# Two DMAs in place of four for the rows of maxima, and the last attention quad in an order of its own

## The chip, the cores and the metric

The kernel runs on one core of a Trainium2 chip. The metric is the device time of one execution in microseconds (us). TensorE (PE; PEld is its weight load), VectorE (DVE), ScalarE (ACT), GpSimd (POOL) and the DMA queue of SyncE (SP) each work through their own instructions in the order in which they were written, and wait for one another only through semaphores.

## The reference, cut to what matters

One transformer block on x, 2048 tokens of 576 features, in float32:

```python
mod = (silu(c) @ w_mod).reshape(1, 6, 1, -1)            # sa, ca, ga, sb, cb, gb
h = layernorm(x) * (1 + ca) + sa
q = (h @ wq) as 32 heads of 18;  k = h @ wk;  v = h @ wv    # one key and value head for all
p = softmax(q k^T * 18 ** -0.5);  x = x + ga * (p v as 576 features) @ wo
h = layernorm(x) * (1 + cb) + sb
x = x + gb * (gelu(layernorm(h) @ w1 + b1) @ w2 + b2)       # w1 is 576 x 4608
```

## The kernel before, in words

Numbers are kept as pairs: a value is rounded to the matmul type (the high part), and the rest (the low part) is a tile of its own; a product of pairs is three matmuls. All order is written out by hand: each engine executes in the order of the Python code.

**Attention.** The tokens are four blocks (`tb`) of 512; the heads are eight groups of four. One block with one group is a *quad*, so there are 32, numbered `n` from 0. In a quad:

- `st_mm` (L941) makes 64 score matmuls of 128 keys by 512 tokens, for two groups `g` of partitions (tokens S0 and S1 in the tables of order). Their weights are a piece of `KS`, their operand is `QST[n]`, 64 partitions for each group. Each goes to a bank of PSUM, and ACT writes its exponential into `P` (L943).
- `pv_mm` (L931) multiplies a key tile of `P` (four score outputs) with V and adds it up in one bank, `psC`. A token `V4` is one whole key tile, `V3` three quarters of one. It runs two key tiles behind the scores (`LAG`).
- Seven PSUM banks go round in a ring (`bank`). A matmul takes the oldest, or a later one by the number of `+` behind its token, and waits until the bank's last reader is done.
- Softmax needs each row's maximum before its quad begins. The maxima of quad n+1 are found in quad n: score products with the queries as weights (M0, M1, R1 at L327, X1 at L951), reduced by DVE (L963, L961) or passed through ACT (L954). `smax_fin1` (F1) joins them, and `smax_fin2` (F2) turns them with PE (L365), and writes the negated maxima as high and low part into `ms` (ACT L367, DVE L368). DMAs on SP (L372) carry `ms` into two rows of each partition group of `QST[n+1]`, rows 54 and 55 and rows 118 and 119, where the score matmuls add them in. So the first score matmul of a quad waits for these DMAs.
- `post_quad` divides by the softmax's sum in steps: copy `psC` to `O` (ACT L748, as soon as the last `pv_mm` of the quad is issued), then the tokens T1, RC, T2, OS (transpose L751, reciprocal and product L754 and L755, transpose L757, split L767 and L768).
- A token `WO` is an output-projection piece: 14 matmuls (L733) for 128 tokens and half of the features, and an add on DVE (L737). There are 24 for the first three blocks. Quads 9 to 30 have one each, quad 30 has another one at its very end, and the last quad has one. Behind the 24th, `RW` reloads the last block of rows of the output weights (SP L1029), which the last block of tokens uses.

**The last quad** (n = 31) has no maxima to find. Its order is eight times the same pattern of four to six scores and a key tile at a time (`LASTW`, `LAST`).

**After it** come the output products of the last block: `wo_tile(t, k0, k1)` makes 24 matmuls (k 0 to 3) and 6 (k = 4, which needs the last quad's result) for 128 tokens. Tiles 0, 1 and 2 come at once, tile 3 (`rest`) between the first MLP products. At the same time `post_quad` runs for the last quad, on ACT and DVE alone, and `form` makes the MLP's operands from the normalized rows `yr`: for an operand such as T1, `=T1` is a difference of blocks (L1062), `+T1` its high part on ACT (L1069), `-T1` its low part (L1071), on DVE, or on POOL for the last two (T4, B22).

**The MLP** runs 36 rounds `v` (18 pieces of the hidden features for each half of the tokens) with seven products (A11, S2, S3, A12, S1, A22, S4; L1158). ACT and DVE make the gelu of their results (`gelu`, L1167 to L1173); POOL casts it and forms sums for the second layer (`sums`, L1178, L1179, L1234 to L1241), whose products `fc2s` (L1261) start one round later. `b2_scaled` (POOL, L641 and L642) scales the second bias row `b2g`; its first reader in this stage is L694.

Of the kernel before, what the change touches and what calls it, by code (L numbers as in the profile page):

```python
# [8 lines left out]
F32 = mybir.dt.float32  # L9
# [6 lines left out]
NB = 4  # L16
TB = S // NB
NT = TB // 128
KD = 5
NQ = H // 4  # L20
NQT = NB * NQ
# [3 lines left out]
R3 = 3 * DH  # L25
# [7 lines left out]
def block_kernel(ctx: ExitStack, tc, x, wqkv, wo, w1, b1, w2, b2, c, wmod, ident_in, out):  # L33
    nc = tc.nc
    ve, ac, po, pe, sy = nc.vector, nc.scalar, nc.gpsimd, nc.tensor, nc.sync
# [17 lines left out]
    def psB(): return bank() if RING else PS["t"].tile([128, 512], F32, name="psB", bufs=PS["b"])  # L53
# [4 lines left out]
    def bank(rank=0):  # L58

        b = RING.pop(rank)  # L60
        RING.append(b)
        return PS["t"].tile([128, 512], F32, name="bk%d" % b, bufs=1)
# [73 lines left out]
    QST = {}  # L136
# [226 lines left out]
    def smax_fin2(n, rank=0):  # L363
        p = bank(rank) if RING else psB()
        pe.transpose(p[:16, :128], MR.pop(n), ident)  # L365
        ms = pa.tile([16, 2, 128], F32R, name="ms")
        ac.activation(ms[:, 0], p[:16, :128], AF.Copy, scale=-1.0)  # L367
        ve.scalar_tensor_tensor(ms[:, 1], p[:16, :128], -1.0, ms[:, 0].bitcast(F32), op0=ALU.mult, op1=ALU.subtract)  # L368
        for g in range(2):
            for s in range(2):  # L370
                r = 64 * g + R3 + s
                sy.dma_start(QST[n][r:r + 1].rearrange("o p (t c) -> o (p t) c", c=128).bitcast(F32),  # L372
                             ms[8 * g:8 * (g + 1), s].bitcast(F32))


    for t in range(NT):
# [77 lines left out]
    for tb in range(NB):  # L454
        nz = big() if tb + 1 < NB else None
        for i, m in enumerate((4, 0, 1, 2, 3)):
# [27 lines left out]
            if tb < 2:  # L484
                for _ in range(NSTAT[tb][i]):
                    ln1_stats(*stats.popleft())
                for _ in range(NAPPLY[tb][i]):
                    b, t = applies.popleft()
# [15 lines left out]
    WO, YR, ATT, B2 = {}, {}, {}, {}  # L504
# [135 lines left out]
    def b2_scaled(b2g):  # L640
        po.tensor_mul(b2g, b2g, BC[:, 2, :])  # L641
        po.tensor_scalar(b2g, b2g, 2.0, None, op0=ALU.mult)  # L642
        return b2g
# [74 lines left out]
        po.tensor_tensor(R[:, 5:7], R[:, 5:7], R[:, 0:2], op=ALU.add)  # L718
        yield

    def wo_mm(tb, t, h2, p, k0, k1):
        A = ATT[tb]
        cs = slice(288 * h2, 288 * (h2 + 1))
        for k in range(k0, k1):
            w = 128 if k == KD - 1 and tb == NB - 1 else 126
            ah, al = (A[:w, i, 128 * t:128 * (t + 1)] for i in (k, KD + k))
            wh, wl = (WO[i][:w, k, cs] for i in "hl")
            if k < KD - 1 or tb == NB - 1:
                terms = [(ah, wh), (ah, wl), (al, wh)]
            else:  # L730
                terms = [(ah, wh), (al[:5 * DH], wl[:5 * DH])]
            for i, (a, b) in enumerate(terms):
                pe.matmul(p[:, :288], a, b, start=(k == 0 and i == 0), stop=(k == KD - 1 and i == len(terms) - 1))  # L733

    def wo_add(tb, t, h2, p):
        X = XT[:, NT * tb + t, 288 * h2:288 * (h2 + 1)]
        ve.tensor_tensor(X, p[:, :288], X, op=ALU.add)  # L737

    def wo_piece(tb, t, h2, p):
        wo_mm(tb, t, h2, p, 0, KD)  # L740
        wo_add(tb, t, h2, p)
# [137 lines left out]
    def tail_parts(o, tail, d, e=po):  # L879

        e.tensor_tensor(d, tail[:, 0], tail[:, 1], op=ALU.subtract)
        for x, y in ((o[:, :2], tail), (o[:, 2], d)):
# [18 lines left out]
            M1 S1+ S0 M0 S1 M0 V3 R1 S1 M0 M1+ S0 S1+ S0 V4 S1 T2 OS M0 X1++ M0 S1+ M0 WO S0 M1 S0 M1 S0 M1 V3  # L901
            S1 S0 M1 S0 M0 X1 V3 S1 M0 M1+ M0 S1+ S0 V4 M0 S1+ S0 S1 S0+ R1+ M0 V4 S0+ S1 M0 M1++ M1 S0+ V3 S0
            R1 M0+ F1 S1 S0 X1+ V4 M0 S1 M0 S1+ S0+ M1 F2 V3 S0+ R1 S0+ S1 M0 S1 M0 V3 M0 X1 S1 M0+ S1 R1+ S0 V3""".split()
    LASTW = "S0 S1 S0 S1 S0 S1 WO V4 S0 S1 V4".split()
    LAST = "S0 S1 S0 S1 V4 S0 S1 S0 S1 V4".split()
    P, PVt = {}, {}
    posts = []
    fill = deque([late_weights()])
# [1 line left out]
    def step(q):  # L910
        if q:
            try:
                return next(q[0])
            except StopIteration:
                q.popleft()
# [64 lines left out]
    def wo_next(rank):  # L980
        tb, t, h2 = pieces.popleft()
        wo_piece(tb, t, h2, bank(rank))
        for _ in range(2):
            if held[0] == "T":
                held[0] = step(fill)
        if h2 and tb < 2:
            fill.append(ln2_rows(tb, t))

    pq = 0
    for n in range(NQT):  # L990
        ns = [0, 0]
        if n < NQT - 1:
            order = QUADW if n > NQ else QUAD
            if n == NQT - 2:
                order = order + ["WO"]
        else:
            order = []
            for d in range(8):
                order += LASTW + ["RW"] if d == 4 else LAST
                order += {1: ["T1"], 2: ["RC"], 4: ["T2"], 5: ["OS", "V4"]}.get(d, [])  # L1000
        if n < NQT - 1:
            names = [tok[:2] for tok in order]
            kf, kr = (sum(int(tok[1]) for tok in order[:names.index(a)] if tok[0] == "V") // 4 for a in ("F2", "RC"))
            quiet = kf - 2, kf - 1, kr - 1
        for tok in order:
            rank = tok.count("+")
            tok = tok.rstrip("+")
            if tok[0] == "V":
                g = int(tok[1])
                while g:  # L1010
                    i = min(g, 4 - pq % 4)
                    if pq >= LAG:
                        pv_mm(*divmod((pq - LAG) // 4, 16), pq % 4, pq % 4 + i)
                    pq, g = pq + i, g - i
                    if pq % 4 == 0:
                        between(*divmod(pq // 4 - 1, 16))
            elif tok[0] == "S":
                g = int(tok[1])
                st_mm(n, ns[g] // 2, g, ns[g] % 2, rank)
                ns[g] += 1  # L1020
            elif tok in maxima:
                unit = next(maxima[tok], None)
                if unit:
                    mx_mm(*unit, tok[0], int(tok[1]), rank)
            elif tok == "WO":
                wo_next(rank)
            elif tok == "RW":
                for i, w in enumerate("hl"):
                    sy.dma_start(WO[w][:, KD - 1, :].bitcast(F32), woscr[i])  # L1029
            elif tok[0] == "F":  # L1030
                smax_fin1(n + 1) if tok == "F1" else smax_fin2(n + 1, rank)
            elif n:
                if next(posts[0], 0) == 0:
                    posts.pop()
        if n == NQT - 1:
            W1["r"] = per.tile([128, 40, 128], F32R, name="w1a", tag="big", bufs=3)
            load_w1(0, " ".join(OPS) + " tails")
# [36 lines left out]
    form = op_pieces(YR[0], ve)  # L1074
    RING.clear()
    open_ps("3", 4)
    wop = {}

    def wo_tile(t, k0, k1):
        if t not in wop:  # L1080
            p = psA() if t != 2 else None
            wop[t] = [psB()[:, :288] if t == 2 else p[:, h2, :288] for h2 in range(2)], p
        for h2 in range(2):
            wo_mm(NB - 1, t, h2, wop[t][0][h2], k0, k1)
        if k1 == KD:
            o, p = wop[t]
            if p is None:
                for h2 in range(2):
                    wo_add(NB - 1, t, h2, o[h2])
            else:  # L1090
                Xv = XT[:, NT * (NB - 1) + t, :].rearrange("p (a b) -> p a b", a=2)
                ve.tensor_tensor(Xv, p[:, :, :288], Xv, op=ALU.add)

    for t in range(3):
        wo_tile(t, 0, KD - 1)
    todo = deque(("+B11 +T2", "-B11 =T3 +B21 +T3", "-T2 -T3", "-B21"))
    form(todo.popleft())
    for _ in posts.pop():
        form(todo.popleft())
    for w in todo:  # L1100
        form(w)
    pxp.__exit__(None, None, None)
    tl = ctx.enter_context(tc.tile_pool(name="tl", bufs=1, side="right", reuse_waits="tile"))
    TL.append(tl.tile([128, 4, TB], F32R, name="opt"))
    px = ctx.enter_context(tc.tile_pool(name="mx", bufs=1, side="right", reuse_waits="tile"))
    form("+t0 -t0")
    for t in range(3):
        wo_tile(t, KD - 1, KD)
    form("+t1 =T4 =T1 +T1 -t1 -T1")
    rest = deque((3, k, k + 1) for k in range(KD))  # L1110
    B2["b"] = load_b2()
# [233 lines left out]
    def t_(mid=None):  # L1345
        between2[0] = mid
        step(f2)

    def s_():
        step(sm)  # L1350
# [5 lines left out]
                gens.remove(gen)  # L1356

    form = op_pieces(YR[0], po)
    b2_scaled(B2["b"])
    mark = [None]  # L1360

    for v in range(NV):
        nxt = (v + 1) % NG
        if v == NG - 1:
            while fill:
                step(fill)
            form = op_pieces(YR[1], po)

        def more(half="", first="", room=False):

            if v in (0, NG - 1, NG):
                form(first if v == 0 else half if v == NG - 1 else {"+T4": "-T4 +T1 -B22", "-T4": "-T1 -t1"}.get(first, ""))
            elif v > NG + 1 and fill:
                step(fill)
            elif 0 < v < NG and fill and (room or mark[0] != "T" or v == NG - 2):
                mark[0] = next(fill[0], "end")
                if mark[0] == "end":
                    fill.popleft()
            if v == 0 and rest:
                for _ in range(2):  # L1380
                    if rest:
                        wo_tile(*rest.popleft())
                if not rest:
                    wo_end()
# [33 lines left out]
        g_()  # L1418
        s_()
        more("+T3 +B21", "-B22", True)  # L1420
        t_()
        g_()
        bd = psB()
# [95 lines left out]
```

## Time and profile before

| | |
|---|---|
| median of 3 runs | 2237.01 us (2236.53 to 2237.12) |
| profiled execution | 2234.55 us, of which the span from first to last instruction is 2232.4 us |
| score matmuls L941 (attention) | from 128.1 to 1376.4 us |
| first MLP product L1158 | 1392.25 us |
| granted TensorE clock | 0.998 |
| busy | PE 99%, PEld 65%, DVE 86%, ACT 74%, POOL 68% |

In a row of the timeline the first number is the start in us, the second the time until the group's last instruction ends; then come the engine, the line, the operation, `out<-in`, shapes and a count; `[0.56 <-DMA qst<-ms]` is the engine's idle time just before and what ended it. PE ends are modelled, so a busy PE is not PE at its peak. A quad's score matmul takes two rows of 64 partitions in pairs: S0 and S1 run beside each other.

### The profile page before, as it was taken

The page shows a single profiled execution, that of the slowest core. Times are in us where ns is not written, and L with a number is a line of the kernel's source. Part 1 is how long each engine was busy: PE and PEld are TensorE (multiplying, and loading weights), DVE is VectorE, ACT ScalarE, POOL GpSimd, SP SyncE. Part 2 cuts the span into 40 slices and gives each one's busy share as a digit, 9 for nine tenths or more (in the row PEclk, how much of TensorE's full clock was granted, in tenths as well). Part 3 has the DMA queues.
Part 4 walks back from the last instruction along what each step waited for, and adds up shares of the span by engine and source line. Part 5 has one row for each costly group of instructions (what it writes and reads, how often), then busy time and mean ns, then how long its engine had stood idle before and what let it go on. Part 6 is the DMA issues. An engine that isn't in the chain of part 4 may idle for free.

```text
span 2232.4 us, 46436 instructions
## 1 busy us (share of the span) xinstructions
PE 2203.2 (99%) x16806; PEld 1453.9 (65%) x16806; DVE 1927.3 (86%) x3415; ACT 1646.1 (74%) x3145; POOL 1528.5 (68%) x1761
## 2 busy tenths in 40 slices
PE   8999999999999999999999999999999999999999
PEld 6655555544544445444454445888888898988898
DVE  7599999999999999999999982887888878888887
ACT  5579999999999999999999997444444544343443
POOL 6653466666776686687676630888888867877776
PEclk9999999999999999999999999999999999999999
DMA  6232143433333333333333321666666646676663
GB/s 232 86 128 92 38 139 108 142 123 118 124 119 118 114 129 104 106 133 103 109 129 112 126 70 60 200 179 177 180 179 175 191 126 182 182 216 187 179 184 123
DMA packets 184776, 308.01 MB, mean 138 GB/s; under 512 B 19711, under 2 KB 75407, under 8 KB 184549
## 3 DMA queue, kind: packets, MB, share of 16 engines
q1 hardware_dynamic: 184405, 304.91, 43.8%
q8 instruction: 133, 2.18, 0.4%
q14 instruction: 94, 0.77, 0.1%
q10 hardware_dynamic: 144, 0.15, 0.0%
HBM read 200.97 MB, written 93.79 MB: 132 GB/s over the span
## 4 chain that ended last, share of the span: by engine, by line
PE 88%; DVE 2%; POOL 2%; DMA 1%; ACT 1%; issue 0%; SPq 0%; DVEq 0%; POOLq 0%; ACTq 0%
PE psC L931 22%; PE psB L1158 18%; PE psA L1261 16%; PE bk L941 15%; PE bk L327 10%; PE bk L733 2%; PE bk L951 2%; PE psA L1295 1%; DMA qst<-ms 1%; DVE mx L963 1%; PE psA L733 1%; POOL r L802 0%; PE psB L256 0%; POOL r L863 0%; PE bk L365 0%
## 5 line engine op out<-in xcount | busy, mean ns | idle before, releaser
L943 ACT ACTIVATE P<-bk 128x512 f32<-128x512 f32 x2048 | 1066.5, 625 | 44.5 <-PE bk L327 18.4
L963 DVE TENSOR_REDUCE mx<-bk 128x1 f32<-128x512 f32 x1476 | 935.0, 682 | 51.5 <-PE bk L327 38.9
L941 PE MATMUL bk<-qst,KS 64*128 64x512 f32 x2048 | 597.2, 432 | 10.4 <-DMA qst<-ms 7.9
L327 PE MATMUL bk<-KS,qst 64*128 64x512 f32 x1722 | 590.1, 437 | 0.9
L931 PE MATMUL psC<-P,V 128*32 128x256 f32 (+3 forms) x6776 | 572.2, 433 | 1.0 <-ACT O L748 1.0
L941 PEld LDWEIGHTS bk<-qst,KS 64*128 64x128 f32 x2048 | 295.0, 184 | 284.0 <-ACT P L943 159.3
L1158 PE MATMUL psB<-ops,w1a 128*128 128x512 f32 x1512 | 393.8, 396 | 0.2 <-DVE h L1173 0.2
L327 PEld LDWEIGHTS bk<-KS,qst 64*128 64x128 f32 x1722 | 271.8, 184 | 130.3 <-ACT P L943 59.2
L1158 PEld LDWEIGHTS psB<-ops,w1a 128*128 128x128 f32 x1512 | 270.1, 188 | 46.6 <-DVE h L1173 0.6
L931 PEld LDWEIGHTS psC<-P,V 128*32 128x32 f32 x6776 | 152.3, 108 | 192.8 <-issue 158.3
L1267 DVE TENSOR_TENSOR XT<-psA,XT 128x576 f32<-128x576 f32 x330 | 241.7, 753 | 18.6 <-PE psA L1261 13.2
L1261 PEld LDWEIGHTS psA<-w2s,big 128*128 128x128 f32 x1584 | 223.0, 188 | 13.9 <-POOL big L1235 2.5
L1261 PE MATMUL psA<-w2s,big 128*128 128x288 f32 x1584 | 230.5, 294 | 0.0
L1171 ACT ACTIVATE psB<-gs 128x512 f32<-128x512 f32 x144 | 86.7, 602 | 127.9 <-DVE gs L1170 127.8
L1235 POOL TENSOR_TENSOR big<-s,big 128x512 fp32r<-128x512 f32 x132 | 171.0, 1296 | 10.6
L1167 ACT ACTIVATE h<-psB,b1t 128x512 f32<-128x512 f32 x144 | 98.1, 681 | 102.1 <-PE psB L1158 81.4
L961 DVE CUSTOM_DVE_ANT_0 xc<-bk,xc 128x512 f32<-128x512 f32 x246 | 167.3, 680 | 2.8 <-PE bk L327 1.7
L954 ACT ACTIVATE xc<-bk 128x512 f32<-128x512 f32 x246 | 151.4, 616 | 0.1
L768 POOL TENSOR_TENSOR os<-O,os 128x512 fp32r<-128x512 f32 x31 | 39.9, 1288 | 148.6 <-ACT os L767 148.1
L1170 DVE SCALAR_TENSOR_TENSOR gs<-psB,h 128x512 f32<-128x512 f32 x144 | 98.6, 684 | 39.9 <-ACT psB L1168 39.9
L802 POOL TENSOR_TENSOR r<-r,r 128x256 fp32r<-128x256 f32 (+1 forms) x162 | 122.0, 753 | 13.0
L1176 ACT ACTIVATE big<-h 128x512 fp32r<-128x512 f32 x39 | 24.7, 634 | 133.7 <-DVE h L1173 133.7
(219 smaller groups left out, 3277.9 us busy)
## 6 DMA issues: line engine op xcount, KB each, us to landing
w1a<-w1scr SPq DMA_DIRECT2D x252, 256.0 KB
w2s<-w2sum SPq DMA_DIRECT2D x132, 288.0 KB
w1scr<-r SPq DMA_DIRECT2D x126, 256.0 KB
w2s<-w2scr SPq DMA_DIRECT2D x76, 288.0 KB
w2scr<-r SPq DMA_DIRECT2D x72, 288.0 KB
w2sum<-r SPq DMA_DIRECT2D x72, 288.0 KB
qst<-qscr SPq DMA_DIRECT2D x192, 72.0 KB
w1a<-w2scr SPq DMA_DIRECT2D x33, 288.0 KB
```

The lines of the kernel that those rows point to most:

```text
L327: pe.matmul(o, QST[n][64 * g:64 * g + 64, p, 128 * qt:128 * (qt + 1)], KS[64 * g:64 * g + 64, 512 * kb:512 * (kb + 1)], start=True, stop=True)
L802: po.tensor_tensor(o[:, n:2 * n], src, o[:, :n].bitcast(F32), op=ALU.subtract)
L931: pe.matmul(PVt[n][32 * j:32 * (j + 1), cs], V[:, kc, :], t[:, j, cs], start=(kc == 0 and h0 == 0), stop=(kc == 15), skip_group_check=True)
L941: pe.matmul(t, KS[64 * g:64 * g + 64, 128 * kc:128 * (kc + 1)], QST[n][64 * g:64 * g + 64, i, :], start=True, stop=True)
L943: ac.activation(P[n, kc][:, 2 * i + g, :], t, AF.Exp, scale=SCALE)
L954: ac.activation(XC[-1], t, AF.Relu)
L961: ve.tensor_tensor_reduce(c, t, c, 1.0, -3.0e38, ALU.add, ALU.max, o)
L963: ve.tensor_reduce(o, t, axis=AX.X, op=ALU.max)
L1158: pe.matmul(o, x, y, start=(first and i == 0), stop=(i == len(terms) - 1), skip_group_check=True)
L1235: po.tensor_tensor(unit(u, 1), x, unit(u, 0).bitcast(F32), op=ALU.subtract)
L1261: pe.matmul(p[:, i, :288], x[:, ts_], W2S[k][:, y], start=(bool(first) and q == 0), stop=(q == 2), skip_group_check=True)
L1267: ve.tensor_tensor(o, p[:, :, :288], o, op=ALU.add)
```

## The change

Three things change.

**The rows of maxima.** `smax_fin2` issues two DMAs, one for the high and one for the low part; each writes row 54 + s of both partition groups at once.

**The last quad.** Both `WO` pieces that stood at the end of quad 30 and in the last quad stand inside the last quad now, and two tokens `WP` each make 12 of the 24 products of tile 2 of the last block (k 0 to 3, half of the features), added to the rows by DVE; the rest of that tile starts its sum at k = 4. The products with V come in groups of two key tiles or more.

**Between attention and MLP.** The forms of T2, T3 and B21 move behind the last steps of `post_quad`, the products with k = 4 stand ahead of the low parts of T3 and B21, and `b2_scaled` moves from ahead of the MLP into round 0.

```diff
-        for g in range(2):
-            for s in range(2):
-                r = 64 * g + R3 + s
-                sy.dma_start(QST[n][r:r + 1].rearrange("o p (t c) -> o (p t) c", c=128).bitcast(F32),
-                             ms[8 * g:8 * (g + 1), s].bitcast(F32))
+        for s in range(2):
+            r = R3 + s
+            sy.dma_start(QST[n][r:r + 65:64].rearrange("g p (t c) -> g (p t) c", c=128).bitcast(F32),
+                         ms[:, s].bitcast(F32))
...
-    def wo_mm(tb, t, h2, p, k0, k1):
+    def wo_mm(tb, t, h2, p, k0, k1, end=KD, first=0):
...
-                pe.matmul(p[:, :288], a, b, start=(k == 0 and i == 0), stop=(k == KD - 1 and i == len(terms) - 1))
+                pe.matmul(p[:, :288], a, b, start=(k == first and i == 0), stop=(k == end - 1 and i == len(terms) - 1))
...
-    LAST = "S0 S1 S0 S1 V4 S0 S1 S0 S1 V4".split()
+    LAST = """S1 S0 S1 S0 V8 S1 S0 T1 S1 S0 RC S1 S0 WO S0 S1 S0 T2 S1 V5 S1 S0 S1 S0 S1 OS S0 V11 S0 S1 S0 S1 S0
...
+    part = deque((0, 1))
...
-            if n == NQT - 2:
-                order = order + ["WO"]
...
+            elif tok == "WP":
+                h2 = part.popleft()
+                p = psB()
+                wo_mm(NB - 1, 2, h2, p, 0, KD - 1, KD - 1)
+                wo_add(NB - 1, 2, h2, p)
...
-            wo_mm(NB - 1, t, h2, wop[t][0][h2], k0, k1)
+            wo_mm(NB - 1, t, h2, wop[t][0][h2], k0, k1, first=KD - 1 if t == 2 else 0)
...
-    for t in range(3):
+    for t in range(2):
         wo_tile(t, 0, KD - 1)
-    todo = deque(("+B11 +T2", "-B11 =T3 +B21 +T3", "-T2 -T3", "-B21"))
+    todo = deque(("+B11 +T2", "", "", "-B11"))
     form(todo.popleft())
     for _ in posts.pop():
         form(todo.popleft())
-    for w in todo:
-        form(w)
+    form("-T2 =T3 +T3 +B21")
+    for t in range(3):
+        wo_tile(t, KD - 1, KD)
+    form("-T3 -B21")
...
-    for t in range(3):
-        wo_tile(t, KD - 1, KD)
...
-    b2_scaled(B2["b"])
...
         more("+T3 +B21", "-B22", True)
+        if v == 0:
+            b2_scaled(B2["b"])
```

PE where quad 30 ends and the last quad begins. L941 is a score matmul, L931 a product with V (four matmuls of 512 tokens are one key tile), L733 an output piece. Before:

```order
L931 MATMUL psC<-P,V 32x384 x4
L733 MATMUL bk_20642<-wos,big 128x288 x14
L941 MATMUL bk_20659<-qst,KS 128x512
L941 MATMUL bk_20662<-qst,KS 128x512
L941 MATMUL bk_20665<-qst,KS 128x512
L941 MATMUL bk_20668<-qst,KS 128x512
L931 MATMUL psC<-P,V 32x512 x4
L941 MATMUL bk_20676<-qst,KS 128x512
L941 MATMUL bk_20679<-qst,KS 128x512
L941 MATMUL bk_20682<-qst,KS 128x512
L941 MATMUL bk_20685<-qst,KS 128x512
L931 MATMUL psC<-P,V 32x512 x4
```

The same place of the change (lines above the products are one lower, so L733 is L732):

```order
L931 MATMUL psC<-P,V 32x384 x4
L941 MATMUL bk_20579<-qst,KS 128x512
L941 MATMUL bk_20582<-qst,KS 128x512
L941 MATMUL bk_20585<-qst,KS 128x512
L941 MATMUL bk_20588<-qst,KS 128x512
L931 MATMUL psC<-P,V 32x512 x8
L941 MATMUL bk_20602<-qst,KS 128x512
L941 MATMUL bk_20605<-qst,KS 128x512
L941 MATMUL bk_20610<-qst,KS 128x512
L941 MATMUL bk_20613<-qst,KS 128x512
L941 MATMUL bk_20620<-qst,KS 128x512
L941 MATMUL bk_20623<-qst,KS 128x512
```

The output piece ahead of the first scores is gone (it stands behind the last of these rows now), and the two key tiles that quad 30 still owes come together.

PE where the last quad ends and the MLP begins (L1158 is an MLP product). Before:

```order
L941 MATMUL bk_20958<-qst,KS 128x512
L941 MATMUL bk_20961<-qst,KS 128x512
L931 MATMUL psC<-P,V 32x512 x8
L733 MATMUL psA<-wos,big 128x288 x48
L733 MATMUL psB<-wos,big 128x288 x24
L733 MATMUL psA<-wos,big 128x288 x12
L733 MATMUL psB<-wos,big 128x288 x6
L1158 MATMUL psB<-ops,w1a 128x512 x6
```

Of the change:

```order
L732 MATMUL bk_20897<-wos,big 128x288 x12
L941 MATMUL bk_20912<-qst,KS 128x512
L941 MATMUL bk_20915<-qst,KS 128x512
L941 MATMUL bk_20918<-qst,KS 128x512
L941 MATMUL bk_20921<-qst,KS 128x512
L931 MATMUL psC<-P,V 32x512 x16
L732 MATMUL psA<-wos,big 128x288 x60
L732 MATMUL psB<-wos,big 128x288 x6
L1159 MATMUL psB<-ops,w1a 128x512 x6
```

Between the last product with V and the first MLP product there were 90 output products and are 66; the other 24 stand in the last quad, the second twelve of them in the first row here.

POOL from the last quad into the MLP's round 0. Before:

```order
L768 TENSOR_TENSOR os<-O,os 128x512
L641 TENSOR_TENSOR b2g<-b2g,BC 128x576
L642 TENSOR_SCALAR b2g<-b2g 128x576
L1071 TENSOR_TENSOR ops<-yr,ops 128x1024 x2
L1178 CAST gt_21202<-h 128x512
```

Of the change:

```order
L767 TENSOR_TENSOR os<-O,os 128x512
L1072 TENSOR_TENSOR ops<-yr,ops 128x1024 x2
L640 TENSOR_TENSOR b2g<-b2g,BC 128x576
L641 TENSOR_SCALAR b2g<-b2g 128x576
L1179 CAST gt_21144<-h 128x512
```

The two bias instructions stood ahead of the low parts of T4 and B22; they stand between these and the first cast of the gelu now.

More of the change, by code (lines that the diff above doesn't have):

```diff
@@ L903, in block_kernel @@
             R1 M0+ F1 S1 S0 X1+ V4 M0 S1 M0 S1+ S0+ M1 F2 V3 S0+ R1 S0+ S1 M0 S1 M0 V3 M0 X1 S1 M0+ S1 R1+ S0 V3""".split()
-    LASTW = "S0 S1 S0 S1 S0 S1 WO V4 S0 S1 V4".split()
-    LAST = "S0 S1 S0 S1 V4 S0 S1 S0 S1 V4".split()
+    LAST = """S1 S0 S1 S0 V8 S1 S0 T1 S1 S0 RC S1 S0 WO S0 S1 S0 T2 S1 V5 S1 S0 S1 S0 S1 OS S0 V11 S0 S1 S0 S1 S0
+            S1 WO RW S1 S0 S0 S1 S0 S1 V8 S0 S1 S0 S1 S0 S1 V8 S1 S0 S1 S0 S0 S1 WP S0 S1 S0 S1 V8 S0 S1 S0 S1
+            S0 S1 V8 S0 S1 S0 S1 S0 S1 WP S0 S1 S0 S1 V12""".split()
     P, PVt = {}, {}
@@ L993, in block_kernel @@
             order = QUADW if n > NQ else QUAD
-            if n == NQT - 2:
-                order = order + ["WO"]
-        else:
[L997 to L1000, printed above, removed]
+        else:
+            order = LAST
         if n < NQT - 1:
@@ L1008, in block_kernel @@
             if tok[0] == "V":
-                g = int(tok[1])
+                g = int(tok[1:])
                 while g:
```

## Prediction

> **What bounds the kernel now.** I read the page first (the chain that ended last), then the waits, then the timeline around the quad boundaries and from the last quad into the MLP.
>
> ```profile
> PE 88%; DVE 2%; POOL 2%; DMA 1%; ACT 1%; issue 0%; SPq 0%; DVEq 0%; POOLq 0%; ACTq 0%
> ```
>
> PE carries the chain, and the 1% of DMA, about 22 us, stands there beside `qst<-ms`, the rows of maxima. Of all waits only one stops PE itself for long:
>
> ```profile
> PE bk L941 <- DMA qst<-ms: 7.9, 13, 1.4
> ```
>
> Thirteen times, 7.9 us in all, the first score matmul of a quad waits for those rows. The timeline where quad 29 ends shows such a stop, and the chain the DMA that ends it:
>
> ```profile
> 1301.64 2.88 SPq L372 DMA_DIRECT2D qst<-ms  x4
> 1303.78 0.60 ACT L954 ACTIVATE xc<-bk 128x512 f32<-128x512 f32 x1
> 1304.34 0.85 PE L931 MATMUL psC<-P,V 128*32 128x384 f32 x8
> 1305.75 0.46 PE L941 MATMUL bk<-qst,KS 64*128 64x512 f32 x1 [0.56 <-DMA qst<-ms]
> 1306.25 0.60 ACT L943 ACTIVATE P<-bk 128x512 f32<-128x512 f32 x1 [0.41 <-PE bk L327]
> 1306.29 3.22 DVE L963 TENSOR_REDUCE mx<-bk 128x1 f32<-128x512 f32 x5 [0.65 <-PE bk L327]
> ```
>
> ```profile
> 1303.89 1.77 DMA qst<-ms
> ```
>
> Four issues begin at 1301.64, the fourth at about 1303.89, so 0.75 us apart; the fourth lands 1.77 later, at 1305.66, and the score matmul starts at 1305.75. PE had been done at 1305.19. In that gap PE, DVE (0.65) and ACT (0.41) all stand, so it is lost time for all three.
>
> **The rows of maxima: 32 x 2 DMAs less.** With two DMAs the second is issued at 1301.64 + 0.75 = 1302.39 and lands at 1304.16 if it takes the same 1.77. PE ends at 1305.19, so the stop is gone with 1.0 us to spare. What is late next is the matmul's PSUM bank; its last reader is the L954 above, done at 1304.38, so it costs nothing. The price of the new form isn't in the trace: each DMA carries twice the bytes into two partitions. From below I put the 0.75 and 1.77 as they are, from above the two doubled (1.5 and 3.54, a rival below); I take the first, since the cover of 1.0 us swallows more than half of 1.77 again.
>
> How much of the stops comes back? At other boundaries:
>
> ```profile
> 1262.15 2.84 SPq L372 DMA_DIRECT2D qst<-ms  x4
> 1103.17 2.93 SPq L372 DMA_DIRECT2D qst<-ms  x4
> 1106.35 0.85 PE L931 MATMUL psC<-P,V 128*32 128x384 f32 x8
> 1107.33 0.47 PE L941 MATMUL bk<-qst,KS 64*128 64x512 f32 x1
> 1142.71 2.87 SPq L372 DMA_DIRECT2D qst<-ms  x4
> 1222.54 2.93 SPq L372 DMA_DIRECT2D qst<-ms  x4
> 1226.76 0.47 PE L941 MATMUL bk<-qst,KS 64*128 64x512 f32 x1 [0.66 <-ACT P L943]
> ```
>
> The score matmul starts 4.11 us after the issue at 1301.64, 4.16 at 1103.17, 4.22 at 1222.54: a constant of the DMA, whatever the timeline names, so the 0.66 here counts as well. There are 21 such boundaries (at the ends of quads 9 to 29); the other seven stop for about 0.13 (1107.33 less 1107.20), where DVE had layer-norm statistics to do and PE was late by itself. In all 7.9 + 0.66 + 7 x 0.13 = 9.5 us. A check on back-pressure: the quad that began with the short stop, DVE some 0.4 behind, took 1142.71 - 1103.17 = 39.54 from issue to issue; one that began with the long one took 1301.64 - 1262.15 = 39.49. So 0.05 of about 0.42 is given back, one part in eight. **Gain: 0.9 x 9.5 = 8.5 us**, bounds 5.3 (13 x 0.41, ACT's idle time, if ACT were the limit) and 9.5.
>
> **The last quad.** ACT, the chain's PE rows, and the issue of its rows of maxima:
>
> ```profile
> 1340.54 3.54 ACT L943 ACTIVATE P<-bk 128x512 f32<-128x512 f32 x7
> 1345.50 4.03 ACT L943 ACTIVATE P<-bk 128x512 f32<-128x512 f32 x8 [1.42 <-PE bk L941]
> 1380.40 0.60 ACT L748 ACTIVATE O<-psC 128x512 f32<-128x512 f32 x1 [1.20 <-PE psC L931]
> 1340.61 2.86 SPq L372 DMA_DIRECT2D qst<-ms  x4
> ```
>
> ```profile
> 1342.98 2.06 PE bk L733 x14
> 1345.04 0.66 PE bk L941 x4
> 1345.70 1.00 PE psC L931 x8
> 1368.69 1.85 PE psC L931 x16
> 1377.06 3.25 PE psC L931 x15
> 1380.31 6.55 PE psA L733 x48
> 1386.85 3.18 PE psB L733 x24
> 1392.42 1.41 PE psB L1158 x6
> ```
>
> Count from 1342.98, where quad 30's products with V end. Before, the products with V end at 1380.31 (37.3 on) and the MLP starts at 1392.42 (49.4 on). A score costs PE 0.66/4 = 0.165 us, a key tile 1.00 alone and 0.93 in a group of two, an output piece 2.06, twelve products 3.18/2 = 1.6. PE's work in the changed stretch: 64 x 0.165 = 10.6, 18 tiles at 0.95 = 17.1, two pieces 4.1, two half tiles 3.2: 35.0. The cover of the piece that stood first is gone: the rows land at 1340.61 + 0.75 + 1.77 = 1343.13, so PE stands about 0.3. That is 35.3. ACT has 1.1 us of backlog (until 1344.08), 64 exponentials at 4.03/8 = 0.50, two copies at 0.5, and behind its last one PE has a key tile of 1.0: 35.1, and about 0.7 more for places where it runs dry. So both are nearly full and the products with V end about 35.8 on, 1.5 earlier. Then come 66 products, 6.55 + 18 x 0.133 = 8.9, in place of 12.1: the MLP starts 44.7 on, **4.7 us earlier**. They must not wait for the last quad's result:
>
> ```profile
> 1389.28 0.68 DVE L768 TENSOR_TENSOR big<-O,big 128x512 fp32r<-128x512 f32 x1
> ```
>
> That step ended 9.0 us after the copy (1381.00) with five forms of about 1.2 in between. Four of them move behind it, so it takes about 4.2, 40.7 on, and the products with k = 4 come at 42.4.
>
> **POOL and DVE behind it.**
>
> ```profile
> 1383.24 1.22 DVE L1062 TENSOR_TENSOR yr<-yr 128x1024 f32<-128x1024 f32 x1
> 1394.31 2.33 DVE L1062 TENSOR_TENSOR yr<-yr 128x1024 f32<-128x1024 f32 x1
> ```
>
> ```profile
> 538.05 1.42 POOL L641 TENSOR_TENSOR b2g<-b2g,BC 128x576 f32<-128x576 f32 x1 [6.24 <-DMA b2g<-in_b]
> 539.56 1.68 POOL L642 TENSOR_SCALAR b2g<-b2g 128x576 f32<-128x576 f32 x1
> 1393.97 1.59 POOL L641 TENSOR_TENSOR b2g<-b2g,BC 128x576 f32<-128x576 f32 x1 [21.24 <-DMA b2g<-in_b]
> 1395.65 2.52 POOL L642 TENSOR_SCALAR b2g<-b2g 128x576 f32<-128x576 f32 x1
> 1399.25 4.75 POOL L1071 TENSOR_TENSOR ops<-yr,ops 128x1024 fp32r<-128x1024 f32 x2 [1.08 <-ACT ops L1069]
> 1405.97 0.61 POOL L1178 CAST gt<-h 128x512 fp32r<-128x512 f32 x1 [1.97 <-PE psB L1158]
> 1411.14 1.29 POOL L1237 TENSOR_TENSOR s<-h 128x512 f32<-128x512 f32 x1 [0.62 <-DVE h L1173]
> ```
>
> ```profile
> 1414.49 1.75 PE L1261 MATMUL psA<-w2s,big 128*128 128x288 f32 x12
> ```
>
> ```profile
> 1411.11:1431.96 20.85, 20.85 (x121) 18.56 (x122) 18.10 (x29) 10.84 (x19) 19.82 (x21) 1.00 0.66 198
> ```
>
> Before, `b2_scaled` filled a hole in POOL. Now it stands between the low part of B22 and the first gelu cast, and POOL's time there is wanted. From the end of the last result's copy (1381.00) to the end of `=T1` DVE took 15.6 us, 1.1 of them because that difference ran beside L642 and took 2.33 where 1.22 is usual; the set of DVE instructions up to there is the same in the change, so 14.5. From there to the end of B22's low part it was 1404.00 - 1396.64 = 7.4. Copy done 36.5 on, so POOL has B22 58.4 on. Then `b2_scaled`, not seen at this place: 3.2 (538.05 to 541.24) or 4.2 (1393.97 to 1398.17); I take 3.2, since nothing like L1062 runs on DVE then. Then the casts and the first sum with its two parts, 1405.97 to 1414.48 less 1.2 idle, 7.3: 68.9 on. PE wants that sum for its first second-layer product; that was 71.5 on (1414.49) and would be 66.8 on. So PE waits 2.1 there. **Net gain: 2.6, taken as 2.5**, bounds 0.5 (the dearer `b2_scaled`, and PE and ACT not so full) and 4.7 (no wait). The last row is the round behind: POOL (fifth pair, 19.82 of 20.85) has 1.0 us of slack and PE is back by the same 2.1, so the wait comes once.
>
> The Trainium skill (SBUF — State Buffer, section "Who interferes with whom") says that a DVE instruction with two SBUF inputs and a POOL instruction that reads SBUF lock each other out for a whole instruction, and that one with a single SBUF input does not. Rows 2.33 against 1.22 and 2.52 against 1.68 agree. By that rule `b2_scaled` beside the gelu's DVE steps, which have one input in PSUM, costs the lower price; by the row next to it in time it costs 4.2 and the net is 1.5.
>
> **Sum.** 8.5 + 2.5 = 11.0. The profiled execution took 2234.55 (2232.4 of span and 2.15 around it), so 2223.5; the median of the runs is 2.5 above it, 2237.0, so **2226.0 us**.
>
> **The rivals.**
>
> *Back-pressure* (0.19): without the stop PE runs into ACT or DVE and gets 5.3 us or less of the 9.5. For it: the idle 0.41 of ACT. Against: 39.54 against 39.49. 5.3 + 2.5 = 7.8: 2229.2.
>
> *POOL's new step is hidden* (0.14): the wait at the first second-layer product doesn't come. For it: a DVE chain quicker than its rows. Against: 19.82 of 20.85. 8.5 + 4.7 = 13.2: 2223.8.
>
> *The longer DMAs* (0.05), which ends slower: 8 KB into two partitions take longer to issue and to land. The price at doubled values: 1.5 + 3.54 + 0.09 = 5.13 from issue to score matmul in place of 4.11, 21 x 1.02 = 21.4 lost, less 2.5: 2255.9. It decides from an interval of 4.11; up to 3.55 (1305.19 less 1301.64) it costs nothing. For it: no row shows this form. The Trainium skill (DMA: Bandwidth & Descriptors, section "Why a DMA increments its semaphore by 16 and not by 1") says that a DMA is spread over the largest number of engines up to 16 that divides the slowest dimensions of both sides: 8 for the old form, 2 for the new one, so eight pieces in a row on each of two. By that rule the landing grows by the pieces alone, which the spare time should cover; no run here shows it yet.
>
> *The change doesn't touch the wait* (0.05): the stops come from the bank, as the timeline has it at 1226.76. Then only the tail gains: 2234.5.
>
> **How the numbers follow.** The forecast as it stands has 0.57. The range takes in back-pressure and the hidden step with their bounds: at best 9.5 + 4.7 = 14.2, 2222.8; at worst 5.3 + 0.5 = 5.8, 2231.2. I give 2222.5 to 2231.5, which leaves out the last two rivals and a part of the others. A difference of 0.2%, 4.5 us, is about what a measurement can tell from none. Faster by more: 0.57 + 0.19 + 0.14, 0.90. Within: 0.05. Slower: 0.05.
>
> **What would show it.** Two issues at L372, 0.75 apart; no PE wait for `qst<-ms` over 0.1 but one of about 0.3 at the last quad; the first score about 3.5 us after the first issue; 39.0 us from issue to issue where it was 39.5. The MLP's first product 44 to 45 us after the last of quad 30's products with V; `b2_scaled` at 3.2; and a PE wait of about 2 us ahead of the first L1262. Wrong it would be if the first score still comes 4.1 us after the issue, or if the quads keep their 39.5.

## The result and the profile after

The changed kernel takes 2223.99 us (median of 6 runs, 2221.4 to 2227.06) where the kernel before takes 2236.38 (6 runs, 2235.35 to 2237.12): 12.4 us less, ratio 0.9945, 95% interval 0.9932 to 0.9958. The forecast was 2226.0, in a range of 2222.5 to 2231.5. The profiled execution took 2223.82, 2221.7 of it span.

The chain that ended last, from the page of the changed kernel:

```profile
PE 88%; POOL 2%; DVE 2%; ACT 1%; issue 1%; DMA 0%; POOLq 0%; ACTq 0%
```

DMA's share went from 1% to 0%. The group of the score matmuls, with its idle time behind the second bar, and the timeline at the same place as before, the end of quad 29 (start, duration):

```profile
L941 PE MATMUL bk<-qst,KS 64*128 64x512 f32 x2048 | 596.4, 432 | 1.2 <-DVE mx L345 0.8
```

```profile
1295.76 1.23 SPq L371 DMA_DIRECT2D qst<-ms  x2
1299.26 0.50 PE L941 MATMUL bk<-qst,KS 64*128 64x512 f32 x1
```

No wait for `qst<-ms` is left. The two issues end 1.23 us after the first began; the first score starts 3.50 after it (4.11 before), and its row names no idle time.

What that is worth shows from issue to issue. The rows of maxima for quads 9 and 31, first issue each, of the kernel before (its second row is in the prediction: 1340.61) and of the changed one:

```profile
460.31 2.92 SPq L372 DMA_DIRECT2D qst<-ms  x4
```

```profile
462.80 1.33 SPq L371 DMA_DIRECT2D qst<-ms  x2
1334.23 1.23 SPq L371 DMA_DIRECT2D qst<-ms  x2
```

880.30 us between them before, 871.43 after: **8.87 us**. Behind the last issue, the last quad and the way into the MLP:

```profile
1336.76 0.73 PE L941 MATMUL bk<-qst,KS 64*128 64x512 f32 x4 [0.17 <-ACT P L943]
1393.81 1.43 POOL L640 TENSOR_TENSOR b2g<-b2g,BC 128x576 f32<-128x576 f32 x1
1395.34 1.67 POOL L641 TENSOR_SCALAR b2g<-b2g 128x576 f32<-128x576 f32 x1
1402.88 0.53 PE L1262 MATMUL psA<-w2s,big 128*128 128x288 f32 x2 [0.15 <-POOL big L1235]
1404.23 1.59 PE L1262 MATMUL psA<-w2s,big 128*128 128x288 f32 x10 [0.81 <-POOL big L1236]
```

`b2_scaled` stands where it was put, and PE waits 0.15 and 0.81 for the two parts of the first sum. The chain's own rows give the whole: the first output products behind the last product with V, the first MLP products, the MLP products behind the first second-layer product (called the **anchor** from here on), and the kernel's last output products. After:

```profile
1371.54 8.16 PE psA L732 x60
1380.49 1.41 PE psB L1159 x6
1405.82 1.86 PE psB L1159 x8
2216.70 1.61 PE psB L1296 x12
```

Before, the last two:

```profile
1416.24 1.86 PE psB L1158 x8
2227.12 1.61 PE psB L1295 x12
```

From the last issue of rows (1334.23; 1340.61 before) the MLP starts 46.26 us on, where it was 51.81; the anchor comes 71.59 on, where it was 75.63: **4.04 us**, 1.5 less than the MLP's start won. From the anchor to the end it is 810.88 in both. 8.87 + 4.04 = 12.9.

The two profiled executions differ by 10.7 only, since the changed one was 2.5 us late by quad 9 (462.80 against 460.31). Of that 1.7 came between the first two issues of rows (37.28 us apart against 35.60). In a stretch between them, from 129 to 138 us, the instructions are the same in both kernels, but the granted clock (third value from the end) was 0.62 in the changed kernel's execution

```profile
129.00:138.00 9.00, 8.79 (x39) 4.58 (x41) 7.01 (x12) 7.06 (x14) 0.00 (x0) 0.62 0.87 284
```

and 1.00 in that of the kernel before:

```profile
129.00:138.00 9.00, 8.59 (x54) 3.40 (x53) 8.74 (x16) 8.65 (x18) 0.06 (x1) 1.00 0.90 298
```

The change moves no instruction of that stretch, and the cause of the lower clock stays open (the last experiment comes back to it). So the experiments are read by intervals behind it: from the issue of quad 9 to that of quad 31 (the **boundaries**: 880.30 and 871.43), from there to the anchor (the **tail**: 75.63 and 71.59), and to the kernel's last products (886.51 and 882.47).

### The profile page after: what moved, and what is told of

It reads as the page before. It is cut to its first block, busy times and chain, and to the rows that moved or that the text cites. A ratio compares the mean times of both kernels' runs of the same rounds, so it can differ in the third digit from the quotient of the medians.

```text
span 2221.7 us, 46258 instructions
## 1 busy us (share of the span) xinstructions
PE 2201.1 (99%) x16814; PEld 1457.5 (66%) x16814; DVE 1927.8 (87%) x3417; ACT 1644.4 (74%) x3145; POOL 1525.1 (69%) x1761
## 4 chain that ended last, share of the span: by engine, by line
PE 88%; POOL 2%; DVE 2%; ACT 1%; issue 1%; DMA 0%; POOLq 0%; ACTq 0%
PE psC L931 22%; PE psB L1159 18%; PE psA L1262 16%; PE bk L941 15%; PE bk L327 10%; PE bk L732 2%; PE bk L951 2%; PE psA L1296 1%; DVE mx L963 1%; ACT P L943 1%; PE psA L732 0%; POOL r L801 0%; PE psB L256 0%; POOL r L862 0%; DVE mx L352 0%
## 5 line engine op out<-in xcount | busy, mean ns | idle before, releaser
L941 PE MATMUL bk<-qst,KS 64*128 64x512 f32 x2048 | 596.4, 432 | 1.2 <-DVE mx L345 0.8
L931 PE MATMUL psC<-P,V 128*32 128x256 f32 (+3 forms) x6784 | 569.1, 433 | 0.0
L941 PEld LDWEIGHTS bk<-qst,KS 64*128 64x128 f32 x2048 | 296.7, 185 | 266.0 <-ACT P L943 143.0
L931 PEld LDWEIGHTS psC<-P,V 128*32 128x32 f32 x6784 | 152.7, 108 | 191.6 <-issue 159.3
```

The source lines that it names most:

```text
L931: pe.matmul(PVt[n][32 * j:32 * (j + 1), cs], V[:, kc, :], t[:, j, cs], start=(kc == 0 and h0 == 0), stop=(kc == 15), skip_group_check=True)
L941: pe.matmul(t, KS[64 * g:64 * g + 64, 128 * kc:128 * (kc + 1)], QST[n][64 * g:64 * g + 64, i, :], start=True, stop=True)
```

## The experiments

The theory: a stop at a quad boundary is what the issues in a row on SP and one landing take beyond 3.5 us of cover, and the tail's gain is the earlier start of the MLP less a wait for POOL. Rivals: each DMA costs by its number and not by the cover; the landing decides; the shares belong elsewhere.

### The two DMAs alone

The kernel before with

```diff
-        for g in range(2):
-            for s in range(2):
-                r = 64 * g + R3 + s
-                sy.dma_start(QST[n][r:r + 1]..., ms[8 * g:8 * (g + 1), s]...)
+        for s in range(2):
+            r = R3 + s
+            sy.dma_start(QST[n][r:r + 65:64]..., ms[:, s]...)
```

Expected: 

> The kernel before with the two DMAs alone. Theory (the stop at the quad boundary is the time of four issues and one landing; the profile after shows 8.4 to 8.9 us gained up to the last boundary): 8.5 to 9 us less than the kernel before, about 2227.5, no wait for the rows of maxima left in the trace and 3.5 us from first issue to first score at the end of quad 29. Back-pressure as a rival: 5.3 us or less. The rival that the stops come from the PSUM bank: no change.

Measured: 2226.26 us (2225.8 to 2228.32) against 2236.71 before, ratio 0.9956 (0.9943 to 0.997). By the medians that is 10.4 less, more than expected; the intervals in the trace are sharper:

```profile
461.21 1.33 SPq L371 DMA_DIRECT2D qst<-ms  x2
1332.65 1.23 SPq L371 DMA_DIRECT2D qst<-ms  x2
1408.29 1.87 PE psB L1157 x8
```

Boundaries 871.44, as in the changed kernel to 0.01 us, so 8.86 gained by the DMAs alone; tail 75.64, as before. Back-pressure (5.3 or less) and the bank (0) are out.

### The tail alone: four DMAs back

The reverse of that diff on the changed kernel. Expected: 

> The changed kernel with the four DMAs back: the tail alone. Theory: the 21 stops are back, and the tail keeps its gain, taken from the traces as 3.5 to 4 us against the kernel before, about 2232.5. Rival (part of the gain put down to the DMAs is the tail's, or the reverse): under 2 or over 6 us less than before.

Measured: 2234.97 us (2231.86 to 2236.78), ratio 0.9993 (0.9984 to 1.0002): no difference that the times can tell, where about 2232.5 was expected. The intervals say why, with the row of the last quad's first scores and the chain's DMA ahead of it:

```profile
462.36 2.92 SPq L372 DMA_DIRECT2D qst<-ms  x4
1342.73 2.86 SPq L372 DMA_DIRECT2D qst<-ms  x4
1346.82 0.83 PE L942 MATMUL bk<-qst,KS 64*128 64x512 f32 x4 [1.72 <-DMA qst<-ms]
```

```profile
1344.96 1.77 DMA qst<-ms
1415.86 1.86 PE psB L1160 x8
```

Boundaries 880.37, as before; tail 73.13, which is 2.50 less than before and not 3.5 to 4. The expectation left out that the parts depend on each other: the new last quad begins with scores and has lost the output piece that stood ahead of them, so with four DMAs PE stops there for 1.72 us, with two for 0.17. That is the 1.55 between 2.50 and 4.04.

### Three DMAs

The changed kernel with the high parts of both halves in one DMA and the low parts in one each.

```diff
-        for s in range(2):
-            r = R3 + s
-            sy.dma_start(QST[n][r:r + 65:64]..., ms[:, s]...)
+        for s, gs in ((0, (0, 2)), (1, (0, 1)), (1, (1, 2))):
+            r = R3 + s + 64 * gs[0]
+            sy.dma_start(QST[n][r:r + 64 * (gs[1] - gs[0]) - 63:64]..., ms[8 * gs[0]:8 * gs[1], s]...)
```

Expected: 

> The changed kernel with three DMAs: the high parts of both halves together, the low parts apart. Theory (a stop comes only past the cover of 3.5 us): two spacings of 0.65 to 0.75 and 1.77 + 0.09 make 3.2 to 3.4 us from issue to score, so the stop stays away and the time is that of the changed kernel within 1 us. Rival (each issue costs its own time): half of the 8.9 us is back, 4 to 5 us more than the changed kernel.

Measured: 2224.21 us (2222.29 to 2227.89), ratio 0.9948 (0.9935 to 0.996). In the waits of PE two rows matter (total, times, longest):

```profile
PE bk L941 <- DMA qst<-ms: 1.2, 1, 1.2
PE bk L941 <- ACT P L943: 0.9, 1, 0.9
```

Of the 21 boundaries one stopped, for 1.2, and the boundaries took 872.65 (463.29 to 1335.94), 1.22 more than in the changed kernel. So the other 20 cost nothing, though half of the issues taken away are back: the price is not by the DMA, and up to the cover it is zero. The one stop, at the end of quad 28, came from a landing that took 3.14 us, as the chain's row shows; why that one was late stays open.

```profile
1258.82 3.14 DMA qst<-ms
```

The second row of waits is the last quad, whose cover is shorter: its scores came 2.53 us after the issue in the changed kernel (1336.76 less 1334.23), and three DMAs don't fit into that. The anchor comes 72.34 after the last issue, 0.75 later.

### Eight DMAs

The changed kernel with each of the four rows in two halves (`QST[n][r:r + 1, p]`, p of 2, from four partitions of `ms`). Expected: 

> The changed kernel with eight DMAs, each of the four rows in two halves of 2 KB. Theory (issue time in a row on SP): seven spacings of 0.65 to 0.75 and 1.86 make 6.4 to 7.1 us from issue to score, a stop of 2.9 to 3.6 at the 21 boundaries, nine tenths of it lost: 55 to 68 us more than the changed kernel, and up to 31 us on top if the first nine boundaries have no more cover. Rival (it is the landing, and DMAs issued in a row land together): not over the four DMAs' loss, 9 us.

Measured: 2289.88 us (two runs), ratio 1.0239 (1.022 to 1.0258), 66 more than the changed kernel. The issues and the first score at the end of quad 29, the chain's DMA there, and the wait in total:

```profile
1354.74 5.17 SPq L374 DMA_DIRECT2D qst<-ms  x8
1360.47 0.47 PE L944 MATMUL bk<-qst,KS 64*128 64x512 f32 x1 [2.16 <-DMA qst<-ms]
```

```profile
1358.72 1.62 DMA qst<-ms
```

```profile
PE bk L944 <- DMA qst<-ms: 48.6, 23, 3.4
```

The issue time in a row is the theory's; the stop is not. It is 2.2 and not 2.9 to 3.6: the spacing is 0.66 (5.17 less one issue of 0.57, by seven), and the DMA that the first score waited for began to count at 1358.72, six spacings behind the first issue, so the seventh (the eighth brings the other half of the heads, which this score doesn't read), and half the bytes land in 1.62. The 21 boundaries stopped for 44 us in all, but took 58.6 more than in the changed kernel (929.99, from 465.37 to 1395.36). The other 14 go with the clock, as far as the sums tell. Behind the stop of 2.42 us that ended at 1192.37 the windows say

```profile
1192.40:1195.40 3.00, 3.00 (x15) 1.36 (x15) 1.97 (x3) 2.07 (x4) 2.21 (x4) 0.50 0.96 300
```

a granted clock of 0.50, as in the three microseconds after these; windows of 3 us over the whole stretch add up to some 19 us of missing clock, and over the same stretch of the changed kernel to none. So the total fell into the range by luck, for another reason than the one given; the rival (9 us) is out all the same.

### The landing by itself

The changed kernel with three DMAs of 4 KB to a spare tile ahead of the two, so that the two are late:

```diff
+        for g in range(3):
+            sy.dma_start(JUNK[n][8 * g:8 * (g + 1)], ms[:8, 0].bitcast(F32))
         for s in range(2):
```

Expected: 

> The changed kernel with three small DMAs of 4 KB to a spare tile ahead of the two, so that the rows' landing is exposed. Theory with the old landing of 1.77: four spacings of 0.65, 1.77 and 0.14 make 4.5 us from the first issue to the score, a stop of 1.0 at the boundaries and of 2.1 at the last quad, 16 to 22 us more than the changed kernel, and the trace gives the landing of an 8 KB DMA into two partitions itself. By the Trainium skill (DMA: Bandwidth & Descriptors, section Why a DMA increments its semaphore by 16 and not by 1) the new form goes over 2 engines in place of 8 and its landing is the longer of the two; then the stop is longer than 1.0 by the same. Rival from the prediction (landing doubled, 3.54): a stop of 2.8 and over 50 us more.

Measured: 2249.29 us (two runs, 2246.28 and 2252.30), ratio 1.0058 (1.004 to 1.0076), 25 more than the changed kernel where 16 to 22 were expected; from the issue of quad 9 to that of quad 31 it is 892.09, 20.7 more. At the end of quad 29:

```profile
1317.11 1.21 SPq L376 DMA_DIRECT2D qst<-ms  x2
1319.67 0.47 PE L946 MATMUL bk<-qst,KS 64*128 64x512 f32 x1 [1.24 <-DMA qst<-ms]
```

```profile
1317.78 1.76 DMA qst<-ms
```

A DMA of 8 KB into two partitions lands in 1.76 us, one of 4 KB into one in 1.77: the new form costs nothing more. With 0.67 to the second issue and 0.14 behind the landing the first score can start 2.56 after the first of two issues; its cover is 3.50, so the change has 0.94 to spare at a boundary, and nothing in the last quad (2.53). The stop of 1.24 in place of 1.0 comes from the spare DMAs, 0.74 apart (the first began at 1314.88) and not 0.65. By the Trainium skill (DMA: Bandwidth & Descriptors, section "Why a DMA increments its semaphore by 16 and not by 1") the new form is spread over 2 engines and the old over 8. That this makes the landing longer was the expectation's own step, and the two landings, 1.76 and 1.77, don't bear it out.

### b2_scaled ahead of the rounds

```diff
+    b2_scaled(B2["b"])
     mark = [None]
...
-        if v == 0:
-            b2_scaled(B2["b"])
```

Expected: 

> The changed kernel with b2_scaled where it stood before, ahead of the MLP's rounds. Theory (POOL's 3.2 us sit in front of the first sum, DVE pays 1.1 us if they run beside it): the wait of 0.96 us at the first second-layer product goes, up to 1.1 us come back by the collision with DVE, so from the last issue of rows to the first MLP anchor 70.6 to 71.7 us in place of 71.59, and the same time within a microsecond. Rival (its place costs the whole 3.2): 3 us less.

Measured: 2221.4 us (2221.03 to 2222.11), ratio 0.9934 (0.992 to 0.9947). POOL and DVE at the new place, and the two anchors:

```profile
1380.18 2.52 POOL L641 TENSOR_SCALAR b2g<-b2g 128x576 f32<-128x576 f32 x1
1379.30 3.48 DVE L1072 TENSOR_TENSOR ops<-yr,ops 128x1024 fp32r<-128x1024 f32 x2
```

```profile
1403.30 1.87 PE psB L1159 x8
2214.14 1.60 PE psB L1296 x12
```

From the last issue (1332.42) the anchor comes 70.88 on, 0.71 earlier than in the changed kernel, and the end 0.75 earlier. PE's wait for the sum is gone; DVE's pair of forms took 3.48 us where the changed kernel's took 2.35, beside a POOL step that took 2.52 where 1.67 is usual, so 1.1 of the gain goes back. By the medians this run is 2.6 below the changed kernel, near the rival's 3. But 1.9 of what the two profiled executions differ by lay ahead of quad 9 (460.88 against 462.80), far from this place, and behind it there is no 3.2 to be had.

### b2_scaled behind the first sum

The two lines moved to the end of round 0, behind the first step of `sums`. Expected: 

> The changed kernel with b2_scaled behind the first sum S3 of round 0. Theory: the PE wait of 0.96 us goes and no other comes, 70.6 us from the last issue to the anchor in place of 71.59, 1 us less than the changed kernel. Rival (POOL is late for the next sums by the same 3.2): the wait comes one round later and nothing is won.

Measured: 2227.68 us (2223.57 to 2229.65), ratio 0.9957 (0.9944 to 0.9969). The anchor comes 70.08 after the last issue (1406.00 less 1335.92), 1.5 earlier, and then:

```profile
1407.36 1.29 POOL L1241 TENSOR_TENSOR s<-h 128x512 f32<-128x512 f32 x1
1408.69 0.69 ACT L1168 ACTIVATE h<-psB,b1t 128x512 f32<-128x512 f32 x1 [6.00 <-PE psA L1262]
1412.73 2.15 PE L1262 MATMUL psA<-w2s,gt 128*128 128x288 f32 x12 [2.55 <-DVE XT L1268]
```

```profile
2221.17 1.60 PE psB L1296 x12
```

The same ACT step in the changed kernel:

```profile
1405.45 0.69 ACT L1168 ACTIVATE h<-psB,b1t 128x512 f32<-128x512 f32 x1 [4.45 <-POOL s L1241]
```

The end comes 885.25 after the last issue, 2.8 later than in the changed kernel. The rival was right, and worse than it said: POOL's next sum (L1241) now ends at 1408.65, and ACT writes the sum's input `h` anew only then. The trace names PE as the releaser here, but PE's products had long been going on, and in the changed kernel the same step waits for L1241 by name. It starts 72.77 after the last issue in place of 71.22, and PE stands for 2.55 behind it.

### Without the 24 early products

`WP` out of the last quad's order, the three tiles' products behind it as before (90 there). Expected: 

> The changed kernel without the 24 early output products: they come behind the last product with V, 90 there in place of 66. Theory (ACT and PE both nearly full in the last quad): the products with V end 0.7 to 1.5 us earlier, PE has 3.2 more behind them, and since the wait of 0.96 takes part of it the anchor comes 0.7 to 1.6 us later. Rival (PE alone bounds the last quad): the products with V end 3.2 us earlier, the anchor 0 to 1 us earlier.

Measured: 2225.64 us (2224.05 to 2226.15), ratio 0.995 (0.9935 to 0.9965). DVE and PE behind the last quad:

```profile
1381.39 1.55 DVE L1093 TENSOR_TENSOR XT<-psA,XT 128x576 f32<-128x576 f32 x2 [3.34 <-PE psA L732]
1406.67 1.59 PE L1262 MATMUL psA<-w2s,big 128*128 128x288 f32 x10 [0.81 <-POOL big L1236]
```

```profile
1370.81 6.56 PE psA L732 x48
1408.26 1.87 PE psB L1159 x8
```

The products with V end 37.03 after the last issue (1333.78) against 37.31: only 0.3 earlier for 3.2 us less of PE work. In both kernels ACT's last 45 exponentials follow one another without idle time (22.53 us here, 22.62 in the changed kernel), so ACT bounds the last quad, and the 24 products ride there for almost nothing. In the last quad of the kernel before, ACT had waited for scores three times, 2.5 us in all; in the two new ones no such wait is left:

```profile
ACT P L943 <- PE bk L941: 2.5, 3, 1.4
```

The anchor comes 74.48 on, 2.89 later, not 0.7 to 1.6: PE's wait of 0.81 for the sum did not take a part of the 3.2, because DVE's output add (L1093) waits 3.34 for the later products and holds up the forms behind it, and so POOL and the sum. The 24 early products are worth 2.9 of the tail's 4.04.

### b2_scaled split, and the changed kernel beside it

The run ahead of the rounds pointed at POOL's doubling as what collides with DVE, so ACT does it, a round later (`...` leaves out that the other call of `b2_scaled` keeps its doubling, and that the call in round 0 goes):

```diff
     def b2_scaled(b2g):
         po.tensor_mul(b2g, b2g, BC[:, 2, :])
-        po.tensor_scalar(b2g, b2g, 2.0, None, op0=ALU.mult)
...
+    b2_scaled(B2["b"])
     mark = [None]
...
             s_()
+            if v == 0:
+                ac.activation(B2["b"], B2["b"], AF.Copy, scale=2.0)
```

Expected: 

> The changed kernel with b2_scaled taken apart: the product with the scale vector on POOL ahead of the rounds, the doubling on ACT at the end of round 0 (same values). Theory (in the run with b2_scaled ahead, the doubling on POOL cost DVE 1.1 us where both ran; the first wait of PE is gone): from the last issue to the anchor 70.1 us in place of 71.59, from the last issue to the end about 881 us in place of 882.5, and no new wait in round 1. Rival (ACT's extra step delays a gelu, as POOL's did behind the first sum): the anchor is early and the end is not.

Expected of the changed kernel beside it: 

> The changed kernel once more, beside the split one. Theory: 882.5 us from the last issue of rows to the end in the trace as before; the two differ by 1 to 1.5 us, which the times can hardly tell, since the granted clock in the first 140 us of a run moves it by as much.

Measured: the split one 2221.63 us (2221.16 to 2223.61), ratio to before 0.9939 (0.9925 to 0.9952); the changed one 2224.10 (2222.99 to 2225.38), ratio 0.9948 (0.9936 to 0.9961). The split one's rows, then the changed one's:

```profile
1333.09 1.23 SPq L371 DMA_DIRECT2D qst<-ms  x2
1379.98 2.51 DVE L1072 TENSOR_TENSOR ops<-yr,ops 128x1024 fp32r<-128x1024 f32 x2
```

```profile
1403.34 1.86 PE psB L1159 x8
2214.54 1.61 PE psB L1296 x12
```

```profile
1334.62 1.23 SPq L371 DMA_DIRECT2D qst<-ms  x2
```

```profile
1406.15 1.87 PE psB L1159 x8
2217.03 1.61 PE psB L1296 x12
```

Anchor 70.25 on against 71.53, end 881.45 on against 882.41. The collision is gone (2.51), 1.28 is won at the anchor, and 0.3 of it goes back later. The medians differ by 2.5; 1.0 of that is shown by the intervals, and 1.4 lay ahead of quad 9 in the two profiled executions (461.60 and 463.03), where no instruction differs. By the intervals it is the best of the three places, by a little.

That 1.4 need not be chance. From 129 to 138 us the granted clock was 0.81 to 1.00 in the profiled executions of the four kernels that have `b2_scaled` ahead of the MLP's rounds (the kernel before, the two DMAs alone, and the two runs with it ahead, whole or split). It was 0.62 to 0.64 in the eight executions of kernels that have it in round 0, both of the changed kernel among them. So its place may cost a microsecond or two there as well; with one or two profiles of each kernel, no run settles whether it does, or how.

## Why the prediction was right

- **The rows of maxima: 8.5 predicted, 8.87 measured**, and by the DMAs alone 8.86. Issue to score 3.50 (3.5 said), issue to issue 1295.76 less 1256.81, the issue a quad before: 38.95 (39.0 said), 0.94 to spare (1.0 said; the spacing of the two is 0.65 and not 0.75, the landing 1.76). The term is 0.4 short because less came back than one part in eight: 0.6 of 9.5.
- **The stop at the last quad: 0.3 predicted, 0.17 measured.** The cover was named; that the tail needs the two DMAs for it, 1.55 us, was not priced and shows only with the four back.
- **The start of the MLP: 4.7 predicted, 5.5 measured** (46.26 from the last issue in place of 51.81). The products with V were put at 35.8 + 2.4 from the last issue and came at 37.31, earlier by about the 0.7 that had been added for places where ACT runs dry. So they gained 2.4 (39.70 before) where 1.5 was said. The 2.5 us that ACT had waited for scores in the last quad before are gone; the prediction came near this from ACT's total work, without naming these waits. The 24 products behind it were priced at 3.2; taking them back costs 2.9.
- **POOL's step: 3.2 predicted, 3.2 measured** (1393.81 to 1397.01), so the lower price was the right end. In the gelu's stretch nothing collided, and where it did (b2_scaled ahead: 2.52 and 3.48) the Trainium skill's rule (SBUF — State Buffer, section "Who interferes with whom") and the rows agree again.
- **The wait at the first second-layer product: 2.1 predicted, 0.96 measured.** This is the mis-sized term. The sum's parts were ready 67.7 after quad 30's products with V (1404.2 less 1336.5; 68.9 said), since the copy of the last result was done 0.7 earlier than said and the forms took 0.35 less. And PE does not stand from the first product on: the first two need the high part alone and ran 0.53 (row 1402.88) while the low part was made. Idle time understates the loss, though, since those 0.53 count as work: from the end of PE's MLP products (1402.73) to the anchor it is 3.09, where the twelve products took 1.75 before. That is 1.3 of the 1.5 lost behind the MLP's start (5.55 less 4.04), and 1.5 came back where the wait was taken away. So the term is 1.3 and not 2.1.
- **Net in the tail: 2.5 predicted, 4.04 measured**, inside its bounds of 0.5 to 4.7. With 8.87 that is 12.9 by the traces and 12.4 by the medians, where 11.0 was forecast; the rest of the distance to 2226.0 is the kernel before, whose median was 0.6 lower this time.
- **Rivals.** Back-pressure fell with 8.86 for the DMAs alone; the hidden step fell with that wait, although its time, 2223.8, lies nearer to the measured 2223.99 than the forecast does. By the time alone it could not have been told from the forecast; the longer DMAs fell with 1.76; that the change doesn't touch the wait fell with the first trace.

## What to carry to other kernels

Ask of a row of small DMAs not how many they are but whether the last one's issue and its landing fit into the work that covers them: three cost next to nothing at the boundaries where four cost 9 us, and eight cost the stops and the clock behind them. Price a wait for a product of several parts by the part that each instruction needs, and price work moved into a stretch by what bounds that stretch (24 products were almost free where ACT was the limit). When two edits share a cover, try each alone: the last quad's order without the two DMAs gained 2.5 where it gained 4.0 with them.

## What the runs showed of the hardware

- The landing of a small DMA from SBUF to SBUF hardly depended on its form within what was tried: 1.77 us for 4 KB into one partition, 1.76 for 8 KB into two, 1.62 for 2 KB. A single one can be late: 3.14 once, with three DMAs. Their issues on SP are 0.65 to 0.75 apart.
- A stop of PE of about two microseconds was at times followed by a halved clock. With eight DMAs, ten of the 22 stops had a granted clock of 0.50 to 0.74 in one of the next windows of 3 us; the shortest of these stops was 1.70 us, while others of 1.66 to 2.29 were followed by 1.00 throughout. The rows delayed had one of 2.34 at the last quad, also followed by 1.00. Stops of up to 1.4 (the kernel before) and of 0.7 to 1.6 (the rows delayed) at the quad boundaries had 1.00 behind them without exception. The Trainium skill (TensorE: Matmul & The Clock Gate, section "HAM oscillation — how this bites in real kernels") warns of gaps over some 3.4 us; here the clock fell behind some gaps half as long. What decides behind which it falls was not tried.
- The idle time in the profile can be less than what a stop costs: at the first second-layer products it was 0.96, and they came to their end 1.3 later, since two products that ran in the middle of the stop count as work with 0.53.
